# An order of 1,206 words: the H3 and S5 layers of one kernel, scheduled anew

## The chip, the cores and the metric

The kernel runs on one core of a Trainium2 chip. Its five engines work side by side, each through its own queue of instructions in order: TensorE (PE in the profile; its weight loads PEld), VectorE (DVE), ScalarE (ACT), GpSimd (POOL) and SyncE (SP). Transfers are issued from SP (hardware queue q1) and from POOL (software queue q0) and share 16 DMA engines. The metric is the device time of one execution in microseconds; a profile gives the span from the first to the last instruction of one execution.

## The reference

Two layers side by side on inputs of 2048 positions by 1024 channels in bfloat16; their outputs are concatenated.

```python
# A: H3. k is shifted by a filter of 4 taps, multiplied by v, convolved over the sequence
k_shift = sum(k_pad[:, t:t+S, :] * shift_k[:, ks-1-t] for t in range(4))
kv = k_shift * v
y = irfft(rfft(kv, 2*S) * rfft(ssm_k, 2*S))[:S] + kv * ssm_D
a = q * y
# B: S5. a diagonal complex recurrence over the 2048 positions
Lam_bar = exp(dt * Lam);  Bu = x @ (((Lam_bar - 1) / Lam)[:, None] * Bmat).T
for t in range(L):
    h = Lam_bar * h + Bu[:, t, :];  hs.append(h)
b = 2 * (hs @ Cmat.T).real + x * Dskip
return concatenate([a, b], axis=-1)
```

## The kernel before

There is no loop over stages. `ORDER` (lines 69 to 148) is a text of 1,206 words, and the program at the end of `full_kernel` reads them one by one: each calls a small function that issues the instructions of one step. So each engine's queue holds its own steps in the order of the words, with nothing reordered later; a step that waits holds everything behind it on its engine.

```python
for word in ["kv_space"] + ORDER.split():
    task, _, slots = word.partition(":")
    task, _, on[0] = task.partition("@")
    for code, n in re.findall(r"([a-z])(\d+)", slots):
        cur.setdefault(code, []).append(int(n))
    f, *args = task.split(".")
    E[f](*map(int, args))
```

A word has a name and indices, then perhaps `@` with the engine or queue it goes to (`@D` is DVE, `@S` SP, `@G` POOL), then perhaps `:` with the home of the tile it makes: `b` and `a` are slots of SBUF rings (2 and 4 KB a partition), `m` and `e` buffers of products, `w` those of twiddle weights, `p` and `d` are banks of PSUM. A tile that takes a home waits until the last readers of the tile before it are done.

Layer A works as a convolution in three stages through HBM, because the transform is split into 128 x 32 points.

- Start: `ld_w` loads the four taps, eight `wb` (PE) and `wbe` (a copy on ACT or DVE) spread them over the partitions. `hl` loads ssm_k, 512 KB each; `hT` (PE, L637) transposes, `hc` (ACT, L642) copies, `hm` (PE, L650) transforms, `he` (ACT, L657) copies, `hst` stores to Ys_h.
- kv: `kp` loads two rows of k into a ring of eight, `vp` loads v; `kvm`, `kva`, `kvb` and `kvc` (DVE, L590, L604, L609, L611) make kv for two rows; `am` (PE, L617) transforms, `ae` (ACT, L622, tile ysb) copies, `ast` stores to Ys_kv. Each half of 1024 channels of each row is stored by itself: 32 `hst` and 32 `ast`.
- Second stage, 16 groups: `lh` and `lk` load a group of Ys_h and Ys_kv (they cut across all rows, so the first waits for the last store), `lw` the weights; `sh` and `sk` (PE, L685), `she` and `ske` (ACT, L693), `pr` (DVE, L699) the product of spectra, `sa` (PE, L713), `sae` (ACT, L720), `vst` stores to Vs.
- Third stage: `vl` loads Vs, `qp` loads q; `a3` (PE, L742), `a3e` (ACT, L748), `qm` (DVE, L752), `ost` stores the output.

Layer B works on 16 tiles of 128 positions.

- `bl` loads a block of B, `bT` (PE, L464) transposes it and `bc` (ACT L479 or DVE L475) copies it to BT. `cx` loads C and `x` loads x with a transposing DMA, from SP only (L486, L489).
- `U.i.jp.jl` (PE, L498): 16 products of 128 x 128 of tile i; `ue` (ACT, L503) copies; `r1`, `r2`, `sc`, `cm`, `r3`, `r4` (DVE, L512, L524, L529, L534, L512, L541) turn the complex recurrence into a real scan, `sc` being the scan over 2,080 elements; `y.i.half.part` (PE, L552 and L557): the output, eight words a tile; `ye` (ACT, L562), `yst` stores.
- A few small steps (`ld_par`, `sm_pre`, `tabA1`, `sin1`, `stt`, `z1` and others) make the tables of rotations from the parameters. `x.0` to `x.15` and all of C must be in SBUF before the steps that read them; the first half of the sixteen `cx` words (`cx.0` to `cx.3`) is read by `y.i.0`, the second by `y.i.1`.

Of the kernel before, what the change touches and what calls it, by code (L numbers as in the profile page):

```python
# [73 lines left out]
bl.4.0@G:b11 bc.5.0 hm.0.5.0:d2 bT.1.1:p0 par_rest bc.1.1@D hm.0.6.0:d0 sin1 bT.4.1:p1 he.0.5.0:b3 bT.5.1:p0 bc.4.1 bl.0.1@G:b10 tabA2 hm.0.5.1:d1
hT.0.3:p1 bc.5.1 hc.0.3:b13 hl.6@G:a10 hT.0.7:p0 hst.0.5.0@G bT.3.0:p1 bl.7.1@G:b9 hc.0.7:b7 hm.0.1.0:d2 kvm.0:m0 he.0.5.1:b2 bT.6.0:p0 bc.6.0@D
kp.1@G sin2 hst.0.5.1@S kva.0 hm.0.6.1:d1 he.0.6.1:b0 bT.4.0:p0 kp.2@S bc.3.0 x.0:b6 bc.4.0@D eo.1 bT.3.1:p1 kvb.0:a0 hT.0.0:p0 he.0.6.0:b3 bc.3.1
hT.0.2:p1 eo.0 kvc.0 am.0.1:d0 bl.2.0@S:b8 hc.0.2:b4 hc.0.0:b5 kvm.2:m0 bT.7.1:p1 bc.7.1 ld_sd@S hl.5@S:a4 bl.2.1@G:b1 bT.2.1:p0 bc.2.1 bT.0.1:p1
bc.0.1@D hT.0.4:p0 kva.2 cx.5.0 eo.2 ae.0.1:b12 hm.0.7.1:d1 hc.0.4:b11 U.0.2.0:p1 hst.0.6.0@S cx.3.0 stt.0 am.0.0:d0 ae.0.0:b1 U.0.2.1 ue.0.2:a6
kvb.2:a2 U.0.0.0:p0 stt.2 he.0.1.0:b2 bT.2.0:p1 bc.2.0 cx.2.1 hm.0.2.1:d0 hm.0.4.1:d2 he.0.7.1:b9 he.0.4.1:b3 U.0.0.1 ue.0.0 vp.2@S:a7 U.0.3.0:p1
U.0.3.1 U.0.1.0:p0 hm.0.0.1:d1 hm.0.0.0:d2 ast.0.0@G he.0.2.1:b8 kvm.4:m0 cx.4.1 ue.0.3 eo.3 vp.1@S:a1 am.1.0:d0 ast.0.1@S rt U.0.1.1 hst.0.4.1@G  # L80
x.1:b10 U.1.2.0:p1 kp.3@S he.0.0.0:b5 cx.1.1 he.0.0.1:b12 hst.0.0.1@S hst.0.7.1@G stt.3 ue.0.1 am.1.1:d2 hst.0.2.1@S U.1.2.1 z1 ae.1.1:b3 hm.0.7.0:d1
U.1.0.0:p0 kva.4 kvb.4:a0 stt.1 U.1.0.1 ue.1.0:a3 hm.0.2.0:d2 cx.3.1 ue.1.2 z2 ae.1.0:b12 U.1.1.0:p0 U.1.1.1 he.0.7.0:b8 x.4:b7 hm.0.3.0:d0 ue.1.1
hl.7@S:a8 U.1.3.0:p1 U.1.3.1 he.0.2.0:b9 kvc.4 am.5.1:d1 ae.5.1:b1 hl.4@G:a5 hst.0.6.1@G ue.1.3 vp.3@S:a9 kvm.6:m0 kva.6 U.4.1.0:p0 hm.0.3.1:d2
U.4.1.1 ast.1.0@S am.5.0:d1 kvc.2 he.0.3.0:b4 kvb.6:a7 ue.4.1:a1 hst.0.3.0@S x.2:b0 U.4.2.0:p1 U.4.2.1 ae.5.0:b12 ue.4.2 ast.1.1@G hT.1.5:p0
hst.0.0.0@G am.4.1:d0 r1.0:m0 r2.0:a6 kvc.6 am.2.0:d1 U.4.3.0:p1 hst.0.1.0@G hst.0.2.0@S r1.1:m0 sc.0 r2.1:a3 he.0.3.1:b13 hc.1.5:b3 ae.2.0:b5 U.4.3.1
hT.1.7:p0 hst.0.7.0@G ast.5.0@S am.7.0:d1 ue.4.3 hc.1.7:b4 hm.0.4.0:d2 U.2.0.0:p1 cx.7.0 cm.0 ae.7.0:b2 hst.0.3.1@S ae.4.1:b8 ast.5.1@S hT.1.2:p0
am.3.1:d1 U.2.0.1 am.2.1:d0 he.0.4.0:b12 ae.3.1:b11 x.3:b9 kp.4@S ast.3.1@S ast.2.0@G ue.2.0:a9 hst.0.4.0@S hc.1.2:b13 am.3.0:d2 ae.3.0:b1 r3.0:m0
hm.1.5.0:d1 r4.0 U.2.3.0:p1 kvm.8:m0 U.2.3.1 ue.2.3 kva.8 U.2.2.0:p0 sc.1 cx.0.1 hT.1.1:p1 hc.1.1:b5 U.2.2.1 ue.2.2 ae.2.1:b11 am.4.0:d2 ae.4.0:b12
U.3.0.0:p1 U.3.3.0:p0 ast.3.0@S U.3.0.1 cx.7.1 ue.3.0:a2 he.1.5.0:b1 U.3.3.1 ue.3.3 cx.0.0 cx.1.0 hm.1.5.1:d2 hT.1.3:p1 hm.1.1.1:d0 ast.7.0@G
U.2.1.0:p0 hm.1.7.0:d1 U.2.1.1 ast.4.0@S he.1.5.1:b2 hc.1.3:b3 hm.1.3.0:d2 ast.2.1@S he.1.7.0:b12 cx.2.0 ue.2.1 hT.1.4:p1 hm.1.3.1:d1 y.0.0.0:p0  # L90
hc.1.4:b11 hT.1.0:p1 kvb.8:a0 cx.6.1 hst.1.5.1@S he.1.1.1:b3 r1.2:m0 he.1.3.1:b2 r2.2:a9 y.0.0.1 cm.1 hm.1.4.1:d0 y.0.0.2 ast.4.1@S he.1.3.0:b8 cx.5.1
hm.1.4.0:d1 cx.4.0 y.0.0.3 cx.6.0 hc.1.0:b11 hm.1.7.1:d2 he.1.4.1:b4 hst.1.1.1@S r3.1:m0 he.1.7.1:b3 y.0.1.0:p1 y.0.1.1 hm.1.1.0:d0 am.6.0:d2 kp.5@S
y.0.1.2 ye.0.0:b6 hst.1.3.0@S hst.1.7.0@S he.1.4.0:b5 hst.1.4.1@G ae.6.0:b8 hst.1.5.0@G hst.1.7.1@G hm.1.0.0:d1 he.1.0.0:b12 y.0.1.3 ye.0.1 ast.6.0@G
r4.1 hm.1.0.1:d2 hT.1.6:p0 hc.1.6:b4 kvm.10:m0 kva.10 he.1.0.1:b8 kp.6@S hm.1.2.1:d1 y.1.0.0:p1 y.1.1.0:p0 he.1.2.1:b1 y.1.0.1 y.1.1.1 y.1.0.2
am.6.1:d2 hst.1.4.0@S y.1.1.2 am.7.1:d1 ae.7.1:b11 hst.1.0.0@G x.5:b5 y.1.0.3 ye.1.0:b10 yst.0@G y.1.1.3 ye.1.1 x.7:b3 hst.1.3.1@G vp.4@G:a5 kvb.10:a8
U.4.0.0:p1 ae.6.1:b6 vp.6@S:a6 kp.7@S U.5.2.0:p0 kvc.8 am.9.0:d1 ae.9.0:b12 U.4.0.1 U.5.2.1 ue.4.0 kvm.12:m0 kva.12 hm.1.2.0:d2 he.1.2.0:b2 ast.9.0@S
ue.5.2:a10 U.7.3.0:p1 hm.1.6.0:d1 kvb.12:a7 hm.1.6.1:d2 U.7.3.1 ue.7.3:a4 U.5.3.0:p0 he.1.6.0:b13 U.7.0.0:p1 hst.1.2.1@G he.1.1.0:b12 vp.5@S:a3
he.1.6.1:b4 U.5.3.1 U.7.0.1 lw.0@S:w0 kvc.10 am.10.0:d2 lw.1@S:w1 yst.1@G hst.1.2.0@G vp.7@G:a5 am.11.1:d0 ue.7.0 ue.5.3 U.7.2.0:p1 ae.11.1:b1
U.3.2.0:p0 U.7.2.1 kvm.14:m0 kvc.12 ae.10.0:b2 am.10.1:d1 ast.6.1@G ue.7.2 hst.1.1.0@S ast.7.1@S ae.10.1:b6 am.8.1:d0 am.8.0:d2 hst.1.6.0@G ast.11.1@G
ae.8.0:b10 U.3.2.1 ue.3.2 am.12.0:d1 ae.12.0:b13 U.3.1.0:p1 am.12.1:d2 x.6:b11 U.3.1.1 ae.12.1:b12 kva.14 kvb.14:a6 U.5.1.0:p0 ast.10.1@G ld_G@S  # L100
ue.3.1 am.11.0:d1 ae.11.0:b1 U.5.0.0:p1 U.5.1.1 hst.1.6.1@G ae.8.1:b6 kvc.14 hst.1.0.1@G ue.5.1 U.5.0.1 ue.5.0 am.14.0:d2 am.15.0:d0 ae.15.0:b8
ast.11.0@S U.6.1.0:p0 am.9.1:d1 ast.10.0@S ast.12.1@G ast.12.0@G ast.8.1@S ae.14.0:b4 U.6.1.1 ast.8.0@S am.13.1:d0 ue.6.1:a12 U.6.3.0:p1 sc.2 cm.2:a13
r3.2:m0 r4.2 am.15.1:d2 ae.15.1:b12 lh.2@G:a3 ast.15.0@S U.6.3.1 ue.6.3 y.2.0.0:p0 am.14.1:d2 ae.14.1:b1 ast.14.1@S y.2.0.1 lh.0@S:a8 ae.9.1:b2
ast.9.1@S ae.13.1:b13 y.2.1.0:p1 y.2.0.2 y.2.1.1 am.13.0:d0 ast.15.1@S ae.13.0:b10 y.2.0.3 ye.2.0:b6 sh.2.1:d1 ast.13.1@S lh.3@G:a5 sh.3.1:d2
sh.3.0:d0 r1.3:m0 r2.3 sc.3 lh.1@G:a14 she.2.1:a11 ast.14.0@S y.2.1.2 she.3.0:a6 U.7.1.0:p0 x.10:b1 y.2.1.3 ye.2.1 r3.3:m0 cm.3:a7 r4.3 sh.1.0:d1
# [716 lines left out]
```

## Time and profile before

| | |
|---|---|
| median of 3 runs | 376.51 us (366.58 to 381.77) |
| the profiled execution | 366.73 us, span 364.9 us |
| mean granted clock of PE | 0.990 |
| bytes moved | 91.72 MB, 251 GB/s on the mean |
| packets under 512 B (of 65,069) | 37,698 |
| DMA busy share, SP's queue and POOL's | 51.2% and 34.7% |

A row of a timeline or a chain gives start, duration, engine, line, operation, output <- input and count; a bracket at its end gives the engine's idle time before it and what ended that. In the groups of instructions, the numbers behind the bar are busy time in all, mean ns of one, and idle time before with its releasers.

### The profile page before, as it was taken

The numbers are of one execution on the slowest core, as the hardware profiler recorded it, in microseconds if no ns is written. First come the engines' busy times: TensorE is split into PE (matmuls) and PEld (weight loads), VectorE is DVE, ScalarE is ACT, GpSimd is POOL, SyncE is SP. The second block draws the span as 40 slices with busy tenths as digits, with TensorE's granted clock in tenths as the row PEclk, the third lists the DMA queues.
The fourth block names the chain that finished last, engine by engine and source line by source line (L and its number), as shares of the span: only waits on it lengthen the run. The fifth ranks groups of instructions, "written<-read, shape, count | busy, mean of one in ns | idle before, by whom it ended". The sixth has DMA issues, their size and how long they took to land.

```text
span 364.9 us, 9748 instructions
## 1 busy us (share of the span) xinstructions
PE 339.4 (93%) x4237; PEld 220.5 (60%) x4237; DVE 323.7 (89%) x226; ACT 261.0 (72%) x338; POOL 66.4 (18%) x122
## 2 busy tenths in 40 slices
...
GB/s 277 310 340 267 251 248 248 307 309 261 226 365 293 298 217 324 294 245 192 152 254 90 285 186 276 302 343 260 143 133 18 271 175 320 166 341 331 261 280 196
DMA packets 65069, 91.72 MB, mean 251 GB/s; under 512 B 37698, under 2 KB 41410, under 8 KB 65026
## 3 DMA queue, kind: packets, MB, share of 16 engines
q1 hardware_dynamic: 53666, 51.76, 51.2%
q0 software_dynamic: 11360, 39.33, 34.7%
...
## 4 chain that ended last, share of the span: by engine, by line
PE 49%; DVE 17%; DMA 16%; ACT 9%; issue 6%; POOL 1%; ACTq 0%; POOLq 0%; DVEq 0%; SPq 0%
PE ps_y L552 19%; PE ps_u L498 18%; DVE mt L590 5%; DMA Ys_h<-ysbh 4%; DMA Ys_kv<-ysb 4%; PE ps_a L713 3%; PE ps_a L685 3%; ACT ysbh L657 3%; DVE mt L512 2%; DVE h L529 2%; DMA wts<-a_c_W 2%; PE ps_a L742 2%; DMA l2k<-Ys_kv 2%; DVE mt L604 2%; DMA Vs<-vsb 2%
## 5 line engine op out<-in xcount | busy, mean ns | idle before, releaser
L498 PEld LDWEIGHTS <-BT 128*128 128x128 bf16 x2048 | 119.0, 98 | 20.5 <-issue 11.8
L498 PE MATMUL ps_u<-xT,BT 128*128 128x128 bf16 x2048 | 126.9, 220 | 0.4 <-DMA xT<-in_B_x_dram 0.2
L552 PE MATMUL ps_y<-CT,h 128*128 128x512 bf16 x512 | 125.9, 380 | 1.2 <-ACT ysbh L657 1.2
L552 PEld LDWEIGHTS <-h 128*128 128x128 bf16 x512 | 44.2, 98 | 50.3 <-issue 9.7
L529 DVE TENSOR_TENSOR_SCAN h<-rtab,h 128x2080 bf16<-128x2080 f32 x16 | 71.8, 4486 | 0.2
L503 ACT CAST u<-ps_u 128x512 bf16<-128x512 f32 x64 | 38.3, 601 | 16.2 <-PE ps_u L498 15.3
L562 ACT CAST yo<-ps_y 128x512 bf16<-128x512 f32 x32 | 19.0, 593 | 37.7 <-PE ps_y L552 33.6
L622 ACT CAST ysb<-ps_a 128x1024 bf16<-128x1024 f32 x32 | 32.2, 1037 | 12.6 <-PE ps_a L617 7.9
L699 DVE TENSOR_TENSOR hab<-x,h 128x4096 bf16<-128x4096 bf16 x16 | 36.6, 2288 | 4.5 <-ACT x L693 2.1
L720 ACT CAST vsb<-ps_a 128x1024 bf16<-128x1024 f32 x32 | 31.6, 1023 | 8.3 <-PE ps_a L713 8.3
L512 DVE TENSOR_TENSOR mt<-u,Z 128x4096 bf16<-128x4096 bf16 x16 | 36.6, 2290 | 0.7
L590 DVE TENSOR_TENSOR mt<-kring,wbc 128x2048 bf16<-128x2048 bf16 (+3 forms) x14 | 35.8, 2593 | 1.6 <-DMA kring<-in_A_k_dram 1.6
L512 DVE TENSOR_TENSOR mt<-h,Z 128x4096 bf16<-128x4096 bf16 x16 | 36.7, 2291 | 0.3
L657 ACT CAST ysbh<-ps_a 128x1024 bf16<-128x1024 f32 x32 | 32.5, 1043 | 4.3 <-DMA Ys_kv<-ysb 2.4
L693 ACT CAST x<-ps_a 128x1024 bf16<-128x1024 f32 x32 | 31.8, 1025 | 4.0 <-PE ps_a L685 3.8
L693 ACT CAST h<-ps_a 128x1024 bf16<-128x1024 f32 x32 | 31.5, 1023 | 1.6 <-PE ps_a L685 1.5
L557 PE MATMUL ps_y<-Dd,xT 128*128 128x128 bf16 x128 | 28.1, 219 | 0.0
L650 PE MATMUL ps_a<-hT,F1t 128*128 128x512 bf16 x64 | 20.8, 405 | 3.8 <-ACT ysb L622 3.2
L524 DVE TENSOR_TENSOR h<-mt 128x2048 bf16<-128x2048 bf16 x16 | 19.5, 1220 | 1.4 <-PE ps_y L552 1.1
L173 POOL DMA_DIRECT2D Ys_h<-ysbh x18 | 12.9, 719 | 41.7 <-ACT ysbh L657 41.3
L557 PEld LDWEIGHTS <-xT 128*128 128x128 bf16 x128 | 12.5, 98 | 13.0
L541 DVE TENSOR_TENSOR h<-mt 128x2048 bf16<-128x2048 bf16 x16 | 19.6, 1223 | 0.4
...
## 6 DMA issues: line engine op xcount, KB each, us to landing
Ys_kv<-ysb SPq DMA_DIRECT2D x21, 256.0 KB, 4.8
...
Ys_h<-ysbh POOLq DMA_DIRECT2D x18, 256.0 KB, 5.3
...
Ys_h<-ysbh SPq DMA_DIRECT2D x14, 256.0 KB, 4.6
...
```

Of the source, the lines that this page charges most:

```text
L498: nc.tensor.matmul(pu[:, w, jl, :], BT[:, 2 * jp + jl, w, d, :], xT[:, d, :], start=(d == 0), stop=(d == ND - 1))
L503: nc.scalar.copy(u[:, :, 2 * jp:2 * jp + 2, :], st["pu", i, jp][:])
L512: nc.vector.tensor_mul(m, s_, w_)
L529: nc.vector.tensor_tensor_scan(gf, rtab[:].rearrange("p a j t -> p (a j t)"), gf, 0.0, ALU.mult, ALU.add)
L552: nc.tensor.matmul(py[:], h[:, 1 - w, j, 2:TP], CT[:, j, w, dh * 512:(dh + 1) * 512], start=(j == 0 and w == 0), stop=(j == NJ - 1 and w = ...
L557: nc.tensor.matmul(py[:, dl * P:(dl + 1) * P], st["xT", i][:, d, :], Dd[:, d, :], start=False, stop=False)
L590: nc.vector.tensor_mul(m[:, :, j0:j0 + n, :], a_, wbc[:, j0:j0 + n, :].unsqueeze(1).to_broadcast([P, 2, n, DV]))
L622: nc.scalar.copy(st["ysb", r, u][:], st["pa", r, u][:].rearrange("p e d -> p (e d)"))
L657: nc.scalar.copy(st["yh", f, rp, u][:], st["pa", f, rp, u][:])
L693: nc.scalar.copy(t_[:, c_, :], st["ps", key, gq, c_][:].rearrange("p e d -> p (e d)"))
L699: nc.vector.tensor_mul(st["m2", gq][:], st["x16", gq][:].unsqueeze(2).to_broadcast([P, 2, 2, D]), st["h16", gq][:].unsqueeze(1).to_broadca ...
L720: nc.scalar.copy(vsb[:, gi, :], st["ps", "v", gq][gi][:].rearrange("p e d -> p (e d)"))
```

## The change

Nothing but the text in `ORDER` differs. Both orders hold the same 1,206 words without their engines, queues and homes, so the same products, copies and transfers are made; the places in the order, the `@` and the `:` change. POOL issued 110 of the transferring words and SP 152; after, it is 92 and 170. Among the copies that may go to DVE, seven `bc` and four `wbe` were there; after, five and two. The first loads are others, and ld_w goes from POOL to SP:

```diff
-bl.0.0@S:b1 ld_w@G:a0a3 bT.0.0:p0 wb.7:p1 bc.0.0@D bl.7.0@S:b2 wbe.7@D wb.0:p0 bl.6.1@S:b0 wbe.0@D bT.7.0:p1 bc.7.0@D bT.6.1:p0 ld_par par_T:p1 p32
-hl.0@G:a2 bc.6.1 hl.1@G:a1 exp1 hl.3@G:a6 wb.1:p1 wbe.1@D wb.3:p0 wbe.3 wb.5:p1 wbe.5 bl.1.0@S:b3 bl.3.0@G:b6 dve2 bl.5.1@G:b7 exp2 kp.-1@G hl.2@S:a7
...
+bl.4.0@S:b1 ld_F@G bl.5.1@S:b0 bT.4.0:p1 bc.4.0 bl.3.0@S:b2 bT.5.1:p0 bT.3.0:p1 bc.3.0 bc.5.1@D ld_par par_T:p0 p32 exp1 dve2 bl.7.0@G:b5 ld_w@S:a1a0
+wb.2:p0 hl.1@S:a4 dve3 sm_pre wbe.2 wb.1:p1 wbe.1 wb.5:p0 bl.0.1@S:b6 wbe.5 wb.3:p1 wbe.3 wb.7:p0 wbe.7 sin0 exp2 bl.4.1@G:b7 bT.4.1:p1 bc.4.1
+bT.0.1:p0 bc.0.1 wb.6:p1 rt wbe.6 bT.7.0:p0 bc.7.0 bl.1.0@G:b8 bl.6.1@G:b4 kp.-1@G tabA1:a5a2a7a6 hl.3@S:a9 tabA2 hl.2@S:a3 hl.0@S:a10 hT.0.1:p1
+hc.0.1:b3 hT.0.6:p0 hc.0.6:b9 hT.0.3:p1 hm.0.6.0:d0 cx.1.1 hT.0.2:p0 hc.0.3:b10 hm.0.3.1:d1 hm.0.3.0:d2 bT.6.1:p1 sin2 par_rest hc.0.2:b13 bc.6.1@D
+wb.4:p0 wb.0:p1 wbe.4@D kp.0@S he.0.3.1:b1 bl.0.0@G:b0 sin1 vp.0@S:a1 wbe.0@D kvm.0:m0 bl.5.0@S:b2 he.0.6.0:b7 bl.6.0@G:b11 bT.1.0:p0 kp.1@S bc.1.0
```

The loads on SP around `kp.3` to `kp.5` (the words of other engines between them left out; this is a list of words, not of lines):

```diff
-kp.3@S cx.1.1 hst.0.0.1 hst.0.2.1 cx.3.1 x.4 hl.7 vp.3 ast.1.0 hst.0.3.0 x.2 hst.0.2.0 ast.5.0 cx.7.0 hst.0.3.1 ast.5.1 x.3 kp.4
-ast.3.1 hst.0.4.0 cx.0.1 ast.3.0 cx.7.1 cx.0.0 cx.1.0 ast.4.0 ast.2.1 cx.2.0 cx.6.1 hst.1.5.1 ast.4.1 cx.5.1 cx.4.0 cx.6.0 hst.1.1.1 kp.5
+kp.3@S ast.2.1 hst.0.0.0 cx.7.1 cx.7.0 ast.0.1 hst.0.7.0 cx.5.0 ast.0.0 hst.0.0.1 hst.1.5.0 hst.1.5.1 ast.3.0 cx.4.0 ast.4.0 cx.6.0 cx.5.1 cx.6.1 ast.4.1 cx.3.0 cx.1.0 cx.2.0 cx.3.1 kp.4
+ast.5.0 ast.5.1 x.3 kp.5
```

The last lines, where one tile of y stood behind `r4.14` with another, and now `y.15` stands alone behind `r4.15`:

```diff
-vl.5.1@S:a14 ost.1.1@S y.11.1.2 y.13.0.0:p0 a3e.2.0:a7 a3e.2.1 yst.8@G y.11.1.3 ye.11.1 y.13.0.1 vl.5.0@S:a8 y.13.1.0:p1 vl.6.0@G:a13 vl.6.1@G:a1
...
-a3e.0.0:a2 yst.11@S qm.2 ost.2.1@G y.14.1.3 ye.14.1:b1 y.15.1.0:p0 y.14.0.0:p1 y.15.1.1 y.14.0.1 y.15.1.2 ost.2.0@G a3e.5.1 qm.5 ost.5.0@S ost.5.1@G
-y.14.0.2 a3e.0.1 y.15.1.3 qm.0 ye.15.1 ost.0.1@S ost.0.0@S yst.15@S ost.3.1@G y.14.0.3 ye.14.0 yst.14@S
...
+y.14.1.3 ye.14.1 r4.15 a3.6.1:d0 ost.0.0@S ost.1.0@S yst.13@S yst.14@S y.15.1.0:p1 a3e.3.1 qm.3 ost.3.1@S y.15.0.0:p0 y.15.1.1 ost.1.1@G a3e.6.1
+y.15.0.1 ost.5.1@G y.15.1.2 y.15.0.2 y.15.1.3 y.15.0.3 ye.15.1:b2 qm.6 ost.6.1@S yst.7@S ost.6.0@S ost.3.0@G ye.15.0 yst.15@S
```

Between these, `sc.2` stands ahead of `kvc.14` instead of behind it; `x.9` stands ahead of the last `ast` words and `x.10` behind `lk.2`, where both stood just ahead of `lk.2`; and the words of U, y, sh, sk, sa and pr are interleaved otherwise, with other slots.

144 lines of the change are left out of this document (71 added, 73 removed).

## The prediction

> **What bounds the kernel now.** I read the page's busy line first, then the same engines cut at the places where the work changes, then the chain of waits.
>
> ```profile
> span 364.9 us, 9748 instructions
> PE 339.4 (93%) x4237; PEld 220.5 (60%) x4237; DVE 323.7 (89%) x226; ACT 261.0 (72%) x338; POOL 66.4 (18%) x122
> ```
>
> ```profile
> core 0: us, PE busy (x) PEld busy (x) DVE busy (x) ACT busy (x) POOL busy (x), PEclk, DMA share, GB/s
> 0.00:25.00 25.00, 17.20 (x110) 10.62 (x111) 16.03 (x50) 16.42 (x27) 12.58 (x28) 1.00 0.90 306
> 25.00:100.00 75.00, 65.34 (x793) 51.03 (x791) 74.05 (x55) 67.57 (x92) 8.55 (x17) 0.95 1.08 267
> 100.00:165.00 65.00, 63.62 (x672) 41.76 (x672) 59.88 (x32) 43.89 (x56) 15.41 (x25) 1.00 0.99 290
> 165.00:344.00 179.00, 178.36 (x2578) 110.21 (x2579) 167.84 (x87) 124.92 (x155) 26.01 (x47) 1.00 0.72 224
> 344.00:365.00 21.00, 14.87 (x96) 6.86 (x94) 5.86 (x5) 8.17 (x11) 3.89 (x7) 0.98 0.86 237
> ```
>
> The windows' columns are the stretch, its length, then busy us (instructions) of PE, PE's weight loads, DVE, ACT and POOL, then granted clock, DMA share and GB/s. PE's idle time is length less busy: 7.8 us up to 25, 9.7 from 25 to 100, 1.4 from 100 to 165, 0.6 from 165 to 344, 6.1 behind that; 25.6 in all. From 100 on PE has no gap that counts, while DVE is idle for 5.1 + 11.2 us there. That this busy time is work shows in the chain (start, us, engine, tile, line, count):
>
> ```profile
> 290.27 9.04 PE ps_u L498 x160
> ...
> 355.20 3.68 PE ps_y L552 x17
> ```
>
> 160 products of U run at 9.04/160 = 56.5 ns each and 17 of y at 216 ns, back to back. So a U word (16 products) costs PE 0.90 us and a y word (four products and half the time two short ones) about 0.92. The program does the same products in both orders, so the span is PE's work, 339.4, plus PE's idle time, 25.6. A gain has to come out of the 17.5 us of idle before 100 or the 6.1 at the end; a loss is any new gap. DMA share is about 1 from 25 to 165 and 0.72 after: up to 165 loads and stores are the second limit. The profiled execution took 366.73 us, 1.8 more than its span. The median shown is 376.51 (366.58 to 381.77), so runs spread 4% and the profiled one is near the fastest; I sum against 366.73.
>
> **Part 1, the start.** Before, the first product of the DVE stream, kvm.0, begins at
>
> ```profile
> 25.07 4.42 DVE L590 TENSOR_TENSOR mt<-kring,wbc 128x8192 bf16<-128x8192 bf16 x1
> ```
>
> and the first hT words at
>
> ```profile
> 16.76 1.93 PE L637 MATMUL ps_t<-ident,hk 128*128 128x128 bf16 x16 [1.53 <-ACT wbc L479]
> ```
>
> held there by a scale copy on ACT, not by the four hl tiles. After, hl.1 is the tenth load on SP, with hl.3, hl.2 and hl.0 the 12th to 14th, behind four bl tiles. Words up to hl.0 carry 5.0 MB; at the 306 GB/s of the first window plus 1.5 us of start that is 18 us. Two of the eight wb products (4 and 0), which kvm.0 needs, now stand behind four hT words.
>
> ```profile
> L475 DVE COPY BT<-ps_t 128x1024 bf16<-128x1024 bf16 x7 | 4.8, 689 | 5.1 <-PE ps_t L464 5.1
> ...
> L475 DVE CAST wbc<-ps_a 128x512 bf16<-128x512 f32 x4 | 2.7, 686 | 1.8 <-PE ps_a L415 1.8
> ...
> L479 ACT CAST wbc<-ps_a 128x512 bf16<-128x512 f32 x4 | 2.3, 578 | 0.7 <-PE ps_a L415 0.6
> ...
> L479 ACT COPY BT<-ps_t 128x1024 bf16<-128x1024 bf16 x9 | 9.1, 1040 | 7.0 <-PE ps_t L464 7.0
> ...
> L642 ACT COPY hT<-ps_t 128x1024 bf16<-128x1024 bf16 x16 | 16.3, 1038 | 1.8 <-PE ps_t L637 1.8
> ...
> L415 PE MATMUL ps_a<-hk,ones 1*128 1x512 bf16 x8 | 4.5, 589 | 2.0 <-DMA hk<-in_A_shift_k_dram 1.3 <-DVE p L273 0.3 <-DVE BT L475 0.2
> ```
>
> From 18: one hT at about 1 us, then ACT's four hc copies and a sine of like size one after another (5 x 1.04), then wb.4 and wb.0 at 0.59 and the copy wbe.0 at 0.69: 26.1, with handoffs 26.5. kvm.0 is **1.4 us later** (bounds: 2 earlier, if the hl tiles land by 14.5; 5 later, if POOL's 2.9 MB share the engines evenly and the copies queue). On DVE, bc words fall from seven to five and wbe words from four to two: 4 x 0.69 = 2.8 us leave DVE, all ahead of kvm.0; 2 x 1.04 + 2 x 0.58 = 3.2 go to ACT, which is busy 67.6 of 75 us from 25 to 100. DVE's relief buys nothing while PE is the bound. vp.0 takes slot a1, which the scale row holds until wb.0 is done, so SP stands from about 9 to 26 us with x.0, kp.1 and everything else behind it; POOL's bl loads cover most of that, and I charge nothing, with 3 us as the other end (in-flight bytes end near 23).
>
> **Part 2, kvm.0 to kvc.14** (the last product of the kv path). I counted DVE words between the two in both orders: eight each of kvm, kva, kvb and kvc, three bc, four stt, three r1 and r2, two r3 and r4, all alike; only the scans differ, two before and three after (sc.2 moved ahead). Prices:
>
> ```profile
> L529 DVE TENSOR_TENSOR_SCAN h<-rtab,h 128x2080 bf16<-128x2080 f32 x16 | 71.8, 4486 | 0.2
> ...
> L512 DVE TENSOR_TENSOR mt<-u,Z 128x4096 bf16<-128x4096 bf16 x16 | 36.6, 2290 | 0.7
> ...
> L604 DVE TENSOR_TENSOR mt<-mt 128x4096 bf16<-128x4096 bf16 x8 | 18.3, 2290 | 0.1
> ...
> L590 DVE TENSOR_TENSOR mt<-kring,wbc 128x8192 bf16<-128x8192 bf16 x4 | 17.7, 4423 | 1.6 <-DMA kring<-in_A_k_dram 1.6
> ...
> L524 DVE TENSOR_TENSOR h<-mt 128x2048 bf16<-128x2048 bf16 x16 | 19.5, 1220 | 1.4 <-PE ps_y L552 1.1
> ...
> L609 DVE TENSOR_TENSOR acc<-mt 128x2048 bf16<-128x2048 bf16 x8 | 9.8, 1221 | 0.3
> ...
> L368 DVE SCALAR_TENSOR_TENSOR Z<-tab,nbi 128x128 bf16<-128x128 f32 x8 | 2.8, 350 | 0.0
> ```
>
> So +4.5. Against it stand the two waits for loads of before (last bracket of each row: idle and releaser) and the end of kvc.14:
>
> ```profile
> 103.41 4.42 DVE L590 TENSOR_TENSOR mt<-kring,wbc 128x8192 bf16<-128x8192 bf16 x1 [1.36 <-DMA kring<-in_A_k_dram]
> ...
> 114.42 1.22 DVE L611 TENSOR_TENSOR acc<-acc,v 128x2048 bf16<-128x2048 bf16 x1 [2.94 <-DMA v<-in_A_v_dram]
> ...
> 133.94 1.23 DVE L611 TENSOR_TENSOR acc<-acc,v 128x2048 bf16<-128x2048 bf16 x1
> ```
>
> 1.36 + 2.94 = 4.3 could go since DVE comes later, but kp.5 and vp.4 stand at nearly the same place among the bytes (27.6 and 31.3 MB, against 28.1 and 32.3) and vp.7 later (37.8 against 36.0). I keep half: -2.2. New is bc.2.1 on DVE ahead of kvm.2: its bank is freed by hc.0.4, eleven ACT pieces behind hc.0.2 (24.2 + ten at 1.04 and one of 1.8 = 36.4), then a transpose at 0.9 and handoffs: 37.7, where DVE is at 26.5 + 9.7 = 36.2, so +1.5. kvc.14 ends 1.4 + 4.5 - 2.2 + 1.5 = **5.2 later**, at 140.4 (bounds +1.3 and +15, the second from the rival below).
>
> Moved past on SP are the transposing loads. Between kp.3 and kp.4 stand 11 of them and 11 stores, where before 6 and 10 stood, and between kp.4 and kp.5 1 and 2 where 9 and 8 stood:
>
> ```profile
> 47.16 3.63 SPq L486 DMA_TRANSPOSE CT<-in_B_C_im_dram  x1
> ...
> 77.25 0.57 SPq L172 DMA_DIRECT2D kring<-in_A_k_dram  x1
> ...
> 84.25 3.64 SPq L486 DMA_TRANSPOSE CT<-in_B_C_re_dram  x2
> ...
> 98.83 0.40 SPq L172 DMA_DIRECT2D kring<-in_A_k_dram  x1
> ```
>
> Before, kp.4 to kp.5 (77.25 to 98.83) took 21.6 us for 9 transposes and 8 stores, so 22 transfers of this mix take 26.4. kp.3 waits for hl.4, which waits for r1.0; DVE's words from 26.5 to there sum to 34.8, plus the 1.5, so r1.0 ends at 62.8, kp.3 issues at 63.5, kp.4 at 89.9, and lands 4.6 later (98.83 to 103.41 for kp.5) at 94.5. DVE gets to kvm.8 by a further 34.0 us, at 96.8. Covered by 2.3 us; no charge.
>
> **Part 3, kvc.14 to the first sk.** The transforms of the last kv rows end like this before:
>
> ```profile
> 139.72 1.93 ACT L622 CAST ysb<-ps_a 128x1024 bf16<-128x1024 f32 x2 [0.28 <-PE ps_a L617]
> ...
> 150.21 1.01 ACT L622 CAST ysb<-ps_a 128x1024 bf16<-128x1024 f32 x1 [1.33 <-PE ps_a L617]
> ```
>
> The two copies at 139.72 wait for PE (ps_a, L617), which had kvc.14 since 135.17; two am words at 0.43 (the row of 84.58 in the fence below) put PE there at 138.9, so kvc.14 had 3.7 us of slack. That leaves 5.2 - 3.7 = 1.5. From kvc.14 to the last ysb copy PE has 5 U, 7 am and 5 y words before (12.1 us), and 7 U, 5 am, 4 y and 2 sh after, as ae.15.1 now stands behind ye.2.1 (12.7): +0.6. Every lk load waits for the last store:
>
> ```profile
> 84.58 0.43 PE ps_a L617 x2
> ...
> 157.69 7.24 DMA l2k<-Ys_kv
> ...
> 164.98 0.63 PE ps_a L685 x16
> ```
>
> and sk starts as it lands (a sk or sh word: 0.31). Here x.9 and x.10 stood on SP before lk.2; after, x.9 is earlier and x.10 behind lk.2, but lk waited for the stores, so nothing is won. Ahead of the first sk PE has 64 U, 26 y and 8 sh words instead of 60, 32 and 5: +3.6 - 5.5 + 0.9, so 1.0 us less is done when it waits. PE is behind by 1.5 + 0.6 + 1.0 = **3.1 us**.
>
> **Part 4, the rest and the end.** From 165 to 344 PE idles 0.6; the order can't win there, and could lose some tenths at each of 13 further pr; 0 taken, 4 as the upper bound. At the end one y tile follows r4.15 instead of two (7.4 us instead of 14.9): that frees DVE, which has 11.2 + 15.1 us to spare, and PE's last y, its copy and the last store cost 6.1 as before. Queues: 18 transfers go from POOL to SP (110 and 152 become 92 and 170).
>
> ```profile
> Ys_h<-ysbh POOLq DMA_DIRECT2D x18, 256.0 KB, 5.3
> ...
> Ys_h<-ysbh SPq DMA_DIRECT2D x14, 256.0 KB, 4.6
> ```
>
> POOL's stores of this tile land 5.3 us after issue, SP's 4.6, as a store that nobody waits for: no price either way. The Trainium skill, SBUF — State Buffer, "Who interferes with whom", says that transfers issued from GpSimd can be starved while DVE holds the shared port and that the hardware queue is immune; by it the move would gain. These rows show 0.7 us of it at most; by the rule at its best the load waits still charged would go too, 2.2 us less.
>
> **Sum:** 366.7 + 3.1 = 369.8 us, PE 3.1 later from the first sk to the end.
>
> **Rivals.** *Slower: the transposes in front of kp.4.* At 47.16 one took 3.63 us to issue and at 84.25 two took 3.64; if eleven in a row back up to 2.9 each, the stretch is 11 x 2.9 + 11 x 0.45 = 36.9, kp.4 lands at 105 and DVE waits 8.2 at kvm.8. Less slack already spent, all 8.2 reach the first sk, with y.0.0 (needs cx.3.1) late on PE meanwhile: 369.8 + 8.2 = 378.0. It decides once the eleven take over 2.2 us each on average (1.95 in the 26.4 above). For: DMA share 1.08 from 25 to 100. Against: 21.6 us for 17 transfers. *Faster: U fills PE's early gaps.* Ahead of kvm.6 stand 28 U words instead of 16, ahead of kvm.8 32 instead of 25. If they fill the 9.7 us idle from 25 to 100 and the delays of parts 1 to 3 hide in it, 366.7 - 9.7 + 1.0 = 358.0. Against: PE's words there wait for ACT's copies of the banks, and ACT has 7.4 us left, 3.2 of it taken. *No effect of the order* (every engine finds the same waits): 366.7, inside the forecast's band.
>
> **Numbers.** 2% of 366.7 is 7.3, about what a measurement of this kernel can tell: 359.4 to 374.0 counts as the same. Forecast and no effect 0.50, slower rival 0.33, faster rival 0.17; so faster 0.17, same 0.50, slower 0.33. The forecast's own range is 364 to 374 (kvc.14 early; 4 us in part 4). The range for 8 in 10 is 359 to 380: it takes in the slower rival, and the upper half of the runs' spread shown.
>
> **What would show it.** Right: first DVE kvm (L590) near 26.5; no kring wait at kvm.8; kvc.14's end near 140; the first L685 on l2k near 168; PE idle under 1 us from there to the end. Wrong: a kring wait of over 3 us near 97 (slower rival); PE idle from 25 to 100 under 5 us (faster); a first sk before 163; or PE gaps in the pr stretch, which no row of before shows.

## The result and the profile after

The changed kernel takes 371.58 us in the median of 17 runs (370.17 to 374.33), the kernel before 368.65 in the median of 17 runs beside it (365.18 to 381.77). The ratio is 1.0105, with a 95% interval of 1.0075 to 1.0135: 3.9 us slower on 368.65, less than the 2% that the prediction took as the least that can be told, but told all the same. The two medians as they stand differ by 2.9. The profiled execution took 370.17 us with a span of 368.1, 3.2 more than before. Some executions of both kernels are disturbed and some per cent longer: the ratios leave them out, the medians do not, and of the disturbed traces that e12 and e14 left only the first 25 us of e12 are read.

The page's busy line, and the same stretches as before (columns as in the prediction; the last stretch ends behind the span):

```profile
span 368.1 us, 9738 instructions
...
PE 338.0 (92%) x4237; PEld 219.6 (60%) x4237; DVE 320.4 (87%) x222; ACT 266.9 (73%) x344; POOL 55.3 (15%) x103
```

```profile
core 0: us, PE busy (x) PEld busy (x) DVE busy (x) ACT busy (x) POOL busy (x), PEclk, DMA share, GB/s
0.00:25.00 25.00, 12.97 (x81) 8.54 (x82) 11.57 (x43) 16.81 (x22) 7.57 (x21) 1.00 0.97 272
25.00:100.00 75.00, 65.91 (x790) 50.47 (x788) 69.52 (x54) 70.27 (x100) 7.24 (x12) 0.98 1.01 256
100.00:165.00 65.00, 62.37 (x737) 44.14 (x736) 62.28 (x33) 47.58 (x59) 13.33 (x23) 1.00 0.94 297
165.00:344.00 179.00, 178.77 (x2522) 108.25 (x2520) 164.58 (x87) 124.15 (x153) 23.50 (x41) 1.00 0.74 223
344.00:369.00 25.00, 18.00 (x117) 8.25 (x115) 12.43 (x7) 8.09 (x11) 3.66 (x6) 0.97 0.86 258
```

PE's work fell by 1.4 us and its idle time rose by 4.5, from 25.6 to 30.1. By stretch (length less busy time; the last one to the end of the span): 12.0 us up to 25 (7.8 before), 9.1 from 25 to 100 (9.7), 2.6 from 100 to 165 (1.4), 0.2 to 344 (0.6), 6.1 behind it (6.1). So the loss stands in two places: +4.2 at the start and, from 100 on, 2.6 where before there was only the 1.2 us wait for the first load of lk. DVE has lost its full stretch from 25 to 100 (69.5 busy instead of 74.05) and made that up later, where it had room.

PE's timeline, the rows with the four gaps that matter (start, duration, engine, line, operation and count; in the bracket the idle time ahead and its releaser):

```profile
15.92 1.03 PE L464 MATMUL ps_t<-ident,ld 128*128 128x128 bf16 x8 [4.66 <-DMA ld<-in_B_B_im_dram]
...
21.35 1.93 PE L637 MATMUL ps_t<-ident,hk 128*128 128x128 bf16 x16 [2.28 <-DMA hk<-in_A_ssm_k_dram]
...
103.46 0.59 PE L650 MATMUL ps_a<-hT,F1t 128*128 128x512 bf16 x2 [1.83 <-ACT ysbh L657]
...
113.56 1.05 PE L498 MATMUL ps_u<-xT,BT 128*128 128x128 bf16 x16 [0.80 <-ACT u L503]
```

At 15.92 PE has waited 4.66 us for bl.0.1, at 21.35 another 2.28 for the hl tiles. The three hT words at the start are done at 24.5; before they were at 18.7 (one at 14.22, which the prediction overlooked, and the two of its row at 16.76). At 103.46 and 113.56 it waits for copies of ACT. From there on PE has no gap that counts, not even at the first sk. In the chain of waits the load of lk lands just as PE gets to it:

```profile
162.82 6.63 DMA l2k<-Ys_kv
169.49 0.41 PE ps_a L685 x8
```

DVE's timeline, SP's and ACT's at the places that the prediction named:

```profile
27.68 0.69 DVE L475 COPY BT<-ps_t 128x1024 bf16<-128x1024 bf16 x1 [10.59 <-PE ps_t L464]
...
30.69 4.43 DVE L590 TENSOR_TENSOR mt<-kring,wbc 128x8192 bf16<-128x8192 bf16 x1
...
101.83 4.42 DVE L590 TENSOR_TENSOR mt<-kring,wbc 128x8192 bf16<-128x8192 bf16 x1 [2.69 <-DMA kring<-in_A_k_dram]
...
143.13 1.20 DVE L611 TENSOR_TENSOR acc<-acc,v 128x2048 bf16<-128x2048 bf16 x1
```

```profile
7.17 9.87 SPq L486 DMA_TRANSPOSE CT<-in_B_C_im_dram  x1
...
29.52 0.33 SPq L172 DMA_DIRECT2D v<-in_A_v_dram  x1
...
67.85 0.69 SPq L172 DMA_DIRECT2D kring<-in_A_k_dram  x1
...
95.41 0.58 SPq L172 DMA_DIRECT2D kring<-in_A_k_dram  x1
96.03 0.90 SPq L173 DMA_DIRECT2D Ys_kv<-ysb  x2
105.22 1.24 SPq L489 DMA_TRANSPOSE xT<-in_B_x_dram  x1
```

```profile
102.40 2.84 ACT L657 CAST ysbh<-ps_a 128x1024 bf16<-128x1024 f32 x3 [3.33 <-DMA Ys_kv<-ysb]
```

kvm.0 begins at 30.69, held by bc.6.1, whose transpose stands behind three hT words on PE, and by the scale copies behind that. SP issues cx.1.1 for 9.87 us, with kp.0 behind it until 17.09, and then stands until vp.0's slot is free at 29.52. kp.4 is issued at 95.41, behind the eleven transposing loads, and DVE waits 2.69 us for it at kvm.8 (101.83). The two stores behind kp.4 (ast.5.0 and ast.5.1, 96.03) land late as well: ACT's next copy, he.1.0.0, goes into slot b7, which ast.5.0 empties, and waits 3.33 us for that. Here PE's gap of 1.83 at 103.46 comes from.

### The profile page after: what moved, and what is told of

Same layout as the page of the kernel before. It is cut to its first block, busy times and chain, and to the rows that moved or that the text cites. A ratio compares the mean times of both kernels' runs of the same rounds, so it can differ in the third digit from the quotient of the medians.

```text
span 368.1 us, 9738 instructions
## 1 busy us (share of the span) xinstructions
PE 338.0 (92%) x4237; PEld 219.6 (60%) x4237; DVE 320.4 (87%) x222; ACT 266.9 (73%) x344; POOL 55.3 (15%) x103
## 4 chain that ended last, share of the span: by engine, by line
PE 60%; DMA 14%; issue 10%; DVE 7%; ACT 5%; SPq 2%; POOL 1%; POOLq 0%; ACTq 0%; DVEq 0%
PE ps_u L498 23%; PE ps_y L552 22%; PE ps_a L685 4%; PE ps_a L713 3%; PE ps_a L617 3%; DMA ld<-in_B_B_im_dram 3%; DMA out_dram<-ot 3%; DVE h L529 2%; DMA Ys_h<-ysbh 2%; DMA l2k<-Ys_kv 2%; DVE hab L699 2%; DMA vv<-Vs 2%; DMA Ys_kv<-ysb 2%; PE ps_a L742 2%; DVE mt L512 2%
## 5 line engine op out<-in xcount | busy, mean ns | idle before, releaser
L552 PE MATMUL ps_y<-CT,h 128*128 128x512 bf16 x512 | 129.6, 380 | 0.4 <-ACT hT L642 0.2
L562 ACT CAST yo<-ps_y 128x512 bf16<-128x512 f32 x32 | 18.9, 590 | 28.6 <-PE ps_y L552 26.4
L650 PE MATMUL ps_a<-hT,F1t 128*128 128x512 bf16 x64 | 19.8, 399 | 4.6 <-ACT ysbh L657 4.6
L464 PE MATMUL ps_t<-ident,ld 128*128 128x128 bf16 x128 | 12.3, 258 | 11.7 <-DMA ld<-in_B_B_im_dram 4.7
L173 POOL DMA_DIRECT2D Ys_h<-ysbh x11 | 7.9, 719 | 83.1 <-ACT ysbh L657 82.7
```

What stands on the lines that cost most here:

```text
L552: nc.tensor.matmul(py[:], h[:, 1 - w, j, 2:TP], CT[:, j, w, dh * 512:(dh + 1) * 512], start=(j == 0 and w == 0), stop=(j == NJ - 1 and w = ...
```

## The experiments

Every kernel was timed in five rounds beside the kernel before, whose median was 368.4 in e1 to e4, 368.7 in e5 to e8, 370.8 in e9 to e12 and 368.2 in e13 and e14. Differences in us are therefore taken between ratios, times 368.5; the changed kernel stands at 1.0105. The intervals are 0.7 to 1.4% wide, so a difference of less than some 2 us to the changed kernel can't be told: -0.6, +0.6, 0.0 and -1.5 in the last column are such. The expectations name these theories. L: the loss is PE's wait for late loads at the start. A: it is the copies moved from DVE to ACT, which bounds PE from 20 to 60. S: it is SP's queue ahead of kp.4. D: the end follows DVE's lateness. P: PE is the only bound from 114 on, and only its own gaps count. Q: it is the stores queued behind kp.4.

| run | edit | ratio to before, 95% | against the changed kernel |
|---|---|---|---|
| e1 | four loads behind hl.0 on SP | 1.0022 [0.9981, 1.0062] | -3.1 us |
| e2 | four bc words to DVE | 1.0190 [1.0133, 1.0246] | +3.1 |
| e3 | kp.4, ast.5 up SP's queue | 1.0184 [1.0137, 1.0230] | +2.9 |
| e4 | vp.0 behind x.1 | 1.0108 [1.0071, 1.0145] | +0.1 |
| e5 | kp.4 on POOL | 1.0020 [0.9986, 1.0054] | -3.1 |
| e6 | ast.5 on POOL | 1.0202 [1.0144, 1.0260] | +3.6 |
| e7 | two bc words to DVE | 1.0090 [1.0044, 1.0136] | -0.6 |
| e8 | e1, e5, e6 and three words to DVE | 1.0104 [1.0045, 1.0163] | 0.0 |
| e9 | e1 and e5 | 0.9979 [0.9942, 1.0016] | -4.6 |
| e10 | kp.4 behind ast.5 on SP | 1.0219 [1.0149, 1.0288] | +4.2 |
| e11 | sc.2 behind kvc.14 | 1.0122 [1.0052, 1.0192] | +0.6 |
| e12 | kernel before, three hl tiles late | 1.0067 [1.0014, 1.0120] | +2.5 against before |
| e13 | e1, and kp.4 on SP ahead of cx.7.1 | 1.0064 [1.0028, 1.0101] | -1.5 |
| e14 | kp.4 on SP ahead of cx.7.1 | 1.0101 [1.0059, 1.0143] | -0.1 |

**e1, the loads of the start.**

```diff
 hl.0@S:a10
+kp.-1@S bl.0.0@S:b0 bl.6.0@S:b11 bl.2.0@S:b12
...
-kp.-1@G
-bl.0.0@G:b0
-bl.6.0@G:b11
-bl.2.0@G:b12
```

> The changed kernel with four loads (kp.-1, bl.0.0, bl.6.0, bl.2.0; 1.57 MB) taken from POOL's queue and put on SP right behind hl.0, so that they no longer share the DMA engines with the four hl tiles. Theory L (the loss is PE's wait for late loads at the start): at 290 GB/s 1.57 MB are 5.4 us, so bl.0.1 lands near 12 instead of 15.9 and the first hT stands near 17 instead of 21.35; PE's idle time in 0 to 25 falls from 12.0 by about 4 to that of before (7.8), and the time falls by 3 to 4 us against the changed kernel (371.6), to about 368. Theory A (ACT's copies bound PE from 20 to 60, and the changed kernel gave ACT 3.2 us more of them): PE's idle time only moves from 0-25 to 25-60 and the time stays within 1 us of 371.6. Theory S (SP's queue further on, the eleven transposing loads ahead of kp.4): no change at all, 371 to 372.

The time fell by 3.1 us, the way theory L had it. PE's timeline and DVE's in e1:

```profile
16.49 0.58 PE L415 MATMUL ps_a<-hk,ones 1*128 1x512 bf16 x1 [2.80 <-ACT BT L479]
...
19.78 1.92 PE L637 MATMUL ps_t<-ident,hk 128*128 128x128 bf16 x16 [1.36 <-ACT wbc L479]
...
29.06 4.43 DVE L590 TENSOR_TENSOR mt<-kring,wbc 128x8192 bf16<-128x8192 bf16 x1
```

No gap of PE waits for bl.0.1 or an hl tile any more; what it waits for now is ACT's chain of copies (2.80 and 1.36). The first hT is 1.6 us earlier, kvm.0 too (29.06). Theory S alone, by which the start was without effect, is out. PE keeps that lead, 1.8 us at the row of 113.56 (111.72 here). The profiled execution of e1 took 370.61, 2 us above e1's median of 368.64; it loses the lead again in waits that the changed kernel's trace does not have, 1.32 us for weights at 185.83 and 1.99 for Vs at 352.85. So the trace shows 1.6 of the 3.1 us, and the rest stands on the times alone; e9 less e5 gives 1.5 for the same four loads and e13 less e14 1.4, neither clear of noise by itself. The loads are worth 1.5 to 3 us, and what is left of the 4.2 lost at the start stays with ACT's copies.

**e2, four copies from ACT to DVE.**

```diff
-bc.0.1
+bc.0.1@D
...
-bc.7.0
+bc.7.0@D
...
-bc.1.0
+bc.1.0@D
...
-bc.0.0
+bc.0.0@D
```

> The changed kernel with four copies of transposes (bc.0.1, bc.7.0, bc.1.0, bc.0.0) done by DVE instead of ACT: 4 x 1.04 leave ACT, 4 x 0.69 go to DVE. Theory A (ACT bounds PE from 20 to 60): PE's idle time from 0 to 60 falls by 3 to 4 and the time by as much, to about 368; DVE's kvm.0 is later by up to 2 and kvc.14 too, which costs nothing. Theory L (late loads): PE waits as long for bl.0.1 and for hl.0; the time falls by under 1 us. If DVE's lateness is what carries the loss (theory D), the time grows by 2 to 3 us.

3.1 us slower, which theories A and L both had wrong. PE's timeline shows why:

```profile
36.16 1.05 PE L464 MATMUL ps_t<-ident,ld 128*128 128x128 bf16 x16 [2.23 <-DVE BT L475]
```

bc.1.0 and bc.0.0 stand behind kvm.0 on DVE, so the banks of their transposes come free only after its 4.4 us; PE stands for 2.23 us. The edit tells where a copy may not go and not what ACT costs; e7 was made for that.

**e3, kp.4 and ast.5 further up.**

```diff
+ast.5.0@S ast.5.1@S kp.4@S
 cx.6.0
...
-kp.4@S
...
-ast.5.0@S ast.5.1@S
```

> The changed kernel with kp.4 and the two stores ast.5.0 and ast.5.1 moved up SP's queue, ahead of the last seven of the eleven transposing loads (cx.6.0 and what follows). Theory S: kp.4 issues near 84 instead of 95.4, the 2.7 us wait at kvm.8 goes, slot b7 comes free earlier, so ACT's 3.3 us wait near 102 and PE's 1.83 us gap at 103.5 go too: time 1.5 to 2 us less, near 370. If DVE's wait for kp.4 is what the end follows (theory D), 2.7 us less, near 369. Theories L and A alone: under 0.5 us.

2.9 us slower. The wait at kvm.8 went (99.78, no wait), but SP is served in order: its row of the stores took 7.08 us, waiting for a copy that ACT made at 90, and the cx loads stood behind it. SP's timeline, and PE's at its y words:

```profile
84.33 7.08 SPq L173 DMA_DIRECT2D Ys_kv<-ysb  x3
```

```profile
96.54 0.59 PE L552 MATMUL ps_y<-CT,h 128*128 128x512 bf16 x1 [4.28 <-DVE h L529]
```

PE stood for 4.28 us, put down to DVE's scan; that had ended 0.5 us earlier, while the first of the held cx loads had left SP only 4.6 us before. That it was the cx load fits these rows and isn't shown by more.

**e4, the blocked queue.**

```diff
-vp.0@S:a1
...
 x.1@S:b9
+vp.0@S:a1
```

> The changed kernel with vp.0 (whose slot a1 is held by the scale row until wb.0 is done) moved on SP from behind kp.0 to behind x.1, so that SP no longer stands from 18 to 29.5 us with bl.5.0, kp.1, bl.2.1, bl.1.1, vp.2, x.0 and x.1 behind it. If the blocked queue costs time, the DMA hole of 185 to 238 GB/s between 18 and 36 us fills, x.0 and x.1 issue 10 us earlier, and PE's idle time from 25 to 60 falls by 1 to 3 us with the time. If it costs nothing, as the prediction charged (ACT's copies hold PE there anyway), the time stays within 0.5 us of 371.6, and vp.0 itself, landing near 36, may make DVE wait at kvc.0.

No change (1.0108 and 1.0105). Without vp.0 SP took 8.36 us over the next two bl loads, whose slots were still taken:

```profile
19.23 8.36 SPq L172 DMA_DIRECT2D ld<-in_B_B_im_dram  x2
```

The cost of nothing that the prediction put on vp.0 stands.

**e5, kp.4 alone, from POOL.**

```diff
-kp.4@S
+kp.4@G
```

> The changed kernel with kp.4 issued from POOL, which stands idle there, instead of from SP behind the eleven transposing loads. The 2.7 us wait at kvm.8 goes and DVE runs 2.7 us earlier from 99 to 143. Theory P (from 113 on PE is the only bound and DVE's lateness costs nothing): time within 0.5 us of the changed kernel's 371.6, PE's 1.83 us gap at 103.5 stays. Theory D (the end follows DVE): 2.7 us less, about 369.

One word moved to another queue takes 3.1 us off. Theory P had expected 0.5 at most, theory D 2.7, with PE's gap still there; but PE's gaps went. POOL's timeline, ACT's and the windows of e5:

```profile
60.41 0.55 POOL L172 DMA_DIRECT2D kring<-in_A_k_dram  x1
```

```profile
98.85 1.01 ACT L657 CAST ysbh<-ps_a 128x1024 bf16<-128x1024 f32 x1
```

```profile
100.00:165.00 65.00, 65.00 (x773) 45.48 (x772) 64.33 (x35) 49.19 (x61) 13.32 (x23) 1.00 0.95 298
```

kp.4 leaves at 60.41 and not at 95.41; the stores ast.5 land 5.3 us after their issue instead of 8.2 at the most, with no kp load among them (vp.3, 512 KB from POOL at 97, is there in both); he.1.0.0 starts at 98.85 and not at 102.40; PE's idle time from 100 to 165 is 0.0 instead of 2.6. These rows fit a price that kp.4 took from PE through the stores beside it. Whether it was that or DVE's wait, e5 can't tell, since both went; e10 was made for it. That the gaps belong to kp.4 and not to one execution, other traces bear out: from 100 to 115 PE idles 2.4, 1.5, 2.2 and 2.9 us in e1, e4, e7 and e11, which leave kp.4 on SP as the change has it (2.6 in the changed kernel), and 0.0 in e5 and 0.2 in e9, which issue it from POOL.

**e6, the two stores from POOL.**

```diff
-ast.5.0@S
-ast.5.1@S
+ast.5.0@G
+ast.5.1@G
```

> The changed kernel with the stores ast.5.0 and ast.5.1 issued from POOL instead of from SP behind the eleven transposing loads and kp.4; nothing waits on SP for them. Slot b7 comes free some 8 us earlier, so ACT's 3.3 us wait near 102 and PE's gap of 1.83 at 103.5 go. Theory P (every gap of PE counts in full): 1.8 us less, about 369.8. Theory D (the end follows DVE, whose wait for kp.4 stays): under 0.5 us.

3.6 us slower where 1.8 faster was expected. ACT's wait went (its copy at 99.07). But on SP x.3 had waited behind kp.4 until slot b1 was emptied by ast.5.1 (105.22 in the changed kernel); with that slot free, x.3, kp.5 and a store left within 4 us of kp.4. SP's timeline, DVE's and PE's:

```profile
96.48 0.58 SPq L172 DMA_DIRECT2D kring<-in_A_k_dram  x1
97.23 1.39 SPq L489 DMA_TRANSPOSE xT<-in_B_x_dram  x1
98.72 2.00 SPq L172 DMA_DIRECT2D kring<-in_A_k_dram  x1
```

```profile
105.68 4.42 DVE L590 TENSOR_TENSOR mt<-kring,wbc 128x8192 bf16<-128x8192 bf16 x1 [6.44 <-DMA kring<-in_A_k_dram]
```

```profile
112.38 1.50 PE L498 MATMUL ps_u<-xT,BT 128*128 128x128 bf16 x16 [4.37 <-DMA xT<-in_B_x_dram]
```

kp.4, issued at 96.48, reached DVE at 105.68, 9.2 us later, and PE waited 4.37 us for x.3. A Ys_h store that left in this stretch was late too, and ACT stood longest of all:

```profile
117.92 1.01 ACT L657 CAST ysbh<-ps_a 128x1024 bf16<-128x1024 f32 x1 [9.90 <-DMA Ys_h<-ysbh]
```

The store that it waits for was issued at 100.82. From 102 to 110 the DMA engines were busy throughout (share 1.09) and yet moved only 97 GB/s, where the changed kernel moved 192 at a share of 0.66; why, this trace doesn't tell. So the rate fell as well as the order of the transfers changing, and the 3.6 us can't be split between the two. The wait that was taken away had kept x.3 and kp.5 apart from kp.4.

**e7, only the two copies that stand ahead of kvm.0.**

```diff
-bc.0.1
+bc.0.1@D
...
-bc.7.0
+bc.7.0@D
```

> The changed kernel with only bc.0.1 and bc.7.0 on DVE, the two copies that stand ahead of kvm.0 where DVE waits 10.6 us anyway; the two that stood behind kvm.0 in the run before this stay on ACT. 2.08 us leave ACT at 17 to 21. Theory A (ACT's copies bound PE from 20 to 60): PE is 1.5 to 2 us earlier at 60, time about 369.8. Theory L (loads: bl.0.1 lands at 15.9, hl.0 at 21.3): the first hT still stands at 21.3, ACT is only idle longer ahead of it, time within 0.5 us of 371.6.

1.0090, inside the changed kernel's interval: no change that can be told. Theory A, that the pieces moved from DVE to ACT are the loss, isn't needed; the edit moves two of the bc words, with the loads still late.

**e8, all of these together.** It holds the edits of e1, e5, e6 and e7, with wbe.6@D.

> The changed kernel with all of these: kp.-1, bl.0.0, bl.6.0 and bl.2.0 on SP behind hl.0; kp.4, ast.5.0 and ast.5.1 on POOL; bc.0.1, bc.7.0 and wbe.6 on DVE. With the loads in order ACT's chain of copies comes next (PE waited 2.80 and 1.36 us for it at 16.5 and 19.8), and these three words take 2.6 us off it. Theory P with L and A: 3 (loads) + 1.8 (gap at 103.5) + 1.5 (copies), so about 365.5, below the kernel before (368.4). If PE's earlier finish runs into the loads of lk at the first sk (1.5 us of wait there in the run with the loads in order), about 367.

1.0104, the changed kernel's own ratio, in six runs from 367.3 to 373.1. Its profiled execution (367.31, span 365.4) was the shortest of these, its median not. What in it gives back 4 us wasn't found; the edit of ast.5 that e6 shows to harm is in it, so e9 was made without it. The wait of 1.5 us at the first sk of e1 that the expectation charges isn't there: e1 waits 0.28 us at its first sk (167.86), and 1.32 at 185.83 for weights.

**e9, the two edits that gave 3 us each.** The edits of e1 and of e5.

> The changed kernel with the two edits that each gave 3 us: kp.-1, bl.0.0, bl.6.0 and bl.2.0 on SP behind hl.0, and kp.4 issued from POOL. If the late loads at the start and kp.4 behind the transposing loads are two separate losses on PE, they add: 371.6 - 3.0 - 3.0 = 365.6, 3 us below the kernel before (368.7). If both only fill the same slack ahead of the first sk (whose load then ends last: in the run with the loads in order PE waited for it again), the time stays near 368.

4.6 us, not 6.2. The median is 367.59 beside 370.84 for the kernel before; the ratio 0.9979 reaches past 1, so it is as fast as the kernel before and can't be called faster. The 6.2 counted e1 at its 3.1; against e5 the four loads bring 1.5 here, near the 1.6 of e1's own trace, so no loss between the two edits has to be explained. There is a gap in this trace all the same, in PE's timeline and ACT's:

```profile
68.72 0.59 PE L617 MATMUL ps_a<-acc,F1t 128*128 128x512 bf16 x2 [1.52 <-ACT ysbh L657]
```

```profile
66.75 1.01 ACT L622 CAST ysb<-ps_a 128x1024 bf16<-128x1024 f32 x1 [1.99 <-DMA Ys_h<-ysbh]
```

kp.4 now leaves at 58.25, among the Ys_h stores, and ACT waits 1.99 us for one of them. But that kp.4 makes this gap isn't shown. In e5 it leaves at 60.41 and PE has no such gap, and in e11, where kp.4 leaves on SP as in the changed kernel, the same word of PE has it:

```profile
71.30 0.59 PE L617 MATMUL ps_a<-acc,F1t 128*128 128x512 bf16 x2 [1.17 <-ACT ysbh L657]
```

There too ACT waits for a Ys_h store (1.64 us at 69.32). The gap comes and goes between executions; its cause is open. ACT's wait near 102 isn't gone for good either: with kp.4 away from there, ACT still waits 1.65 us for its Ys_kv store in e9 (99.77) and 2.02 in e13 (102.60), of the 3.33 in the changed kernel.

**e10, kp.4 one place further down, behind the stores.**

```diff
-kp.4@S
...
 ast.5.0@S ast.5.1@S
+kp.4@S
```

> The changed kernel with kp.4 moved on SP from ahead of the stores ast.5.0 and ast.5.1 to right behind them: 1 us later on the queue, so DVE's wait at kvm.8 grows from 2.7 to about 3.7, while the stores leave 0.6 us earlier and have the DMA engines to themselves. Theory Q (the loss was the stores behind kp.4: slot b7 late, ACT waits, PE's gaps of 1.83 and 0.80 at 103 to 114): the gaps shrink to under 1 in all and the time falls by 1.5 to 2.5 us, to about 369.5. Theory D (the loss was DVE's wait for kp.4, carried to the end): 1 us more, about 372.5.

4.2 us slower, against both. SP's, ACT's, DVE's and PE's rows:

```profile
97.21 0.73 SPq L172 DMA_DIRECT2D kring<-in_A_k_dram  x1
100.72 2.01 SPq L489 DMA_TRANSPOSE xT<-in_B_x_dram  x1
```

```profile
99.61 1.01 ACT L657 CAST ysbh<-ps_a 128x1024 bf16<-128x1024 f32 x1 [0.20 <-DMA Ys_kv<-ysb]
```

```profile
106.07 4.42 DVE L590 TENSOR_TENSOR mt<-kring,wbc 128x8192 bf16<-128x8192 bf16 x1 [6.97 <-DMA kring<-in_A_k_dram]
```

```profile
128.98 0.59 PE L617 MATMUL ps_a<-acc,F1t 128*128 128x512 bf16 x2 [4.49 <-DVE acc L611]
```

Theory Q's mechanism fits: ACT waits 0.20 for the store instead of 3.33, and the gap of 1.83 is gone. But kp.4 was issued 1.8 us later and landed 8.9 after that, beside x.3; DVE waited 6.97 and was 4.2 later at kvm.8 than in the changed kernel, and PE then stood 4.49 us for DVE's acc. DVE's lateness does count once it is large enough: 4.2 plus the 1.7 that PE was earlier (gaps of 0.41 and 0.54 instead of 1.83 and 0.80) gave a wait of 4.5, so the changed kernel had some 1.4 us of slack left there (an estimate from these rows).

**e11, sc.2 where it was before the change.**

```diff
-sc.2
...
 kvc.14
+sc.2
```

> The changed kernel with the scan sc.2 put back behind kvc.14 on DVE, as it stood before the change. kvc.14 ends 4.5 us earlier, near 139.8; the last ysb copy, the stores behind it and the loads of lk follow earlier, by up to 4. The prediction charged PE 1.5 us for kvc.14's delay: if that is right, the time falls by 1.5 us, to about 370. Theory P (PE has no gap from 114 to the end, so nothing on DVE there counts): within 0.5 us of 371.6; the first sk finds its load earlier and does not start earlier.

1.0122 against 1.0105: nothing won. kvc.14 ended at 142.05 instead of 144.33:

```profile
140.82 1.23 DVE L611 TENSOR_TENSOR acc<-acc,v 128x2048 bf16<-128x2048 bf16 x1 [0.51 <-DMA v<-in_A_v_dram]
```

That is 2.3 us earlier and not 4.5, since in this execution kvm.8 was 1.15 later and kvc.14 waited 0.51 for its load. This execution had also lost 1.17 us at 71.30 and reached the row of 113.56 at 115.05, so the +0.6 is no price of sc.2. Theory P holds for this as far as the noise allows: nothing is won by an earlier kvc.14.

**e12, the converse in the kernel before.**

```diff
-hl.0@G:a2
-hl.1@G:a1
-hl.3@G:a6
...
 bl.4.1@G:b9
+hl.0@G:a2 hl.1@G:a1 hl.3@G:a6
```

> The kernel before, with hl.0, hl.1 and hl.3 moved on POOL's queue behind kp.-1 and four bl loads (1.83 MB, about 6 us at 300 GB/s), which is what the change did to the hl tiles. Theory L (the hl tiles' landing sets PE's start): the first hT starts near 20 instead of 14.2 to 16.8, PE's idle time in 0 to 25 grows from 7.8 to about 11, the time from 368.5 to about 371.5. If before's start has cover that the changed kernel lacks, the time stays within 1 us of 368.5.

2.5 us slower than before (interval 0.5 to 4.4). Its first hT word, in PE's timeline:

```profile
17.08 0.44 PE L637 MATMUL ps_t<-ident,hk 128*128 128x128 bf16 x2 [3.01 <-DMA hk<-in_A_ssm_k_dram]
```

It waits 3.01 us for an hl tile, where before none waited for one. Two further waits of 0.82 and 0.63 follow, and up to 25 PE idles 10.6 us instead of 7.8. So late hl tiles alone, with the first hT at 17.08 and not at 21.35 as in the changed kernel, cost time in the other kernel too; the interval is too wide to say what part of the 4.2 they are.

**e13 and e14, kp.4 early but on SP.**

```diff
+kp.4@S
 cx.7.1
...
-kp.4@S
```

> The changed kernel with the four loads on SP behind hl.0 and kp.4 kept on SP but ahead of the first of the eleven transposing loads, so that it issues near 70 instead of 58 (POOL) or 95 (the change). If the 2 us that the two edits together lacked were lost because kp.4, issued at 58, shared the DMA engines with the Ys_h stores that ACT then waited for (1.99 us, PE's gap of 1.52 at 68.7), that gap goes and the time is 365.5 to 366.5, about 2.5 us below the kernel before. If something else ends last, it stays at 367.5.

> The changed kernel with only that move of kp.4 on SP, ahead of the first of the eleven transposing loads. If kp.4's place in the order is the cause, whatever queue issues it, PE's gaps at 103 to 114 go and the time is near 368.6, as with kp.4 on POOL. If it was the relief of SP's queue, it stays near 371.6.

e14 is where the changed kernel is (1.0101), e13 1.4 us better than that and 3.1 worse than e9. The 1.5 by which e13 is ahead of the changed kernel isn't clear of noise. So moving kp.4 up on SP isn't shown to gain anything. e13's SP, ACT and PE rows:

```profile
72.00 0.50 SPq L172 DMA_DIRECT2D kring<-in_A_k_dram  x1
```

```profile
81.84 1.01 ACT L622 CAST ysb<-ps_a 128x1024 bf16<-128x1024 f32 x1 [2.02 <-DMA Ys_kv<-ysb]
```

```profile
83.39 1.95 PE L498 MATMUL ps_u<-xT,BT 128*128 128x128 bf16 x32 [1.62 <-ACT u L503]
```

At 72.00 kp.4 goes out right behind two stores; ACT then waits 2.02 us for a Ys_kv store, and PE 1.62 for ACT. A wait stands 7 to 10 us behind kp.4 in the changed kernel (102), in e13 (82) and in e9 (67), but e11 has the last of these with kp.4 elsewhere, and e5 has none, so that it follows kp.4 isn't shown. Whether e5 gained by POOL's queue as such or by the moment at which kp.4 leaves, these runs don't tell: no run issues it from SP near 60, or from POOL near 95.

## Why the prediction came out as it did

The time forecast, 369.8, lies 0.4 below the profiled 370.17 and 1.8 below the median, and the direction of its sum (+3.1, with +3.2 measured in the span and +3.9 by the ratio) is right. Yet it called this no change that can be told, and the parts of its sum are not those that the trace shows: that the sum comes so near is luck.

**The step that failed first: part 1.** The prediction wrote the span as PE's work and PE's idle time, then costed the late loads only through kvm.0 on DVE and gave PE's own idle time at the start no term. That is where 4.2 us arose. Bringing four loads earlier takes 3.1 back by e1's times (1.6 by its trace, 1.5 and 1.4 by e9 and e13), and late hl tiles cost the other kernel 2.5 (0.5 to 4.4, e12). The size of the delay was also short: hl.0 was put at 18 us from 5.0 MB of words up to it, and PE waited for it until 21.35. POOL's queue had by 7.3 us issued three more bl loads (0.79 MB) that stand later in the order but share the engines, and at the window's 272 GB/s the 5.8 MB are 21.3 us; the prediction had POOL's bytes only in its upper bound. kvm.0 came 5.6 later instead of 1.4, 0.6 beyond the upper bound. Right were the costs of nothing for vp.0 (e4) and for the pieces moved between DVE and ACT (e7, two of the bc words).

**The second: kp.4 "covered by 2.3 us; no charge" in part 2.** The stretch from kp.3 to kp.4 took 27.6 us, with 26.4 forecast (26.9, had its prices per transfer been fitted to the whole 21.6 us of before), and the eleven transposes 1.5 us each (16.3 us of SP's rows in all), well under the 2.2 at which the slower rival was to decide. But kp.3 itself was 4.35 late (much of it kvm.0's delay beyond the forecast, 4.2) and kp.4's landing took 6.4 us instead of 4.6, while DVE was only 2.3 late at kvm.8: 4.35 + 1.2 + 1.8 - 2.3 = 5.0, and the cover of 2.3 became a wait of 2.7. The rival had the right place at a third of its price. What neither saw is the way to PE: through ACT, which waits for the stores behind and beside kp.4 (3.33 us, 0.20 in e10 and none in e5), and through DVE's wait only beyond some 1.4 us more (e10). By e5 kp.4's place and queue are worth 3.1 us together; which of the two stays open, as do the waits that e9 and e13 keep for such a store. The rest of part 2 came out: from kvm.0 to the end of kvc.14 113.6 us, 113.9 forecast, though the wait charged at bc.2.1 (1.5) didn't occur and the two waits for k made 3.0.

**The third: part 3's 3.1 us.** kvc.14 ended 9.2 later, at 144.33, and PE still had no gap over 0.25 us between 113.56 and its last y; e11 moved it by 2.3 and won nothing. The three terms (1.5, 0.6, 1.0) were charged where PE, late by itself, had other words to do. The first sk was put near 168 and began at 169.49, its load landing at 169.45.

**How it adds up.** Gains the sum didn't hold make the difference: the wait at the first sk (1.20 before) is gone, idle time from 25 to 100 is 0.6 less, PE's busy time 1.4 less. 4.2 (start) + 2.6 (the gaps at 103 to 114) - 1.2 - 0.6 - 0.6 (other idle time from 100 to 344) - 1.4 = 3.0, and 0.2 of rounding, for the 3.2 of the spans.

**Part 4 and the rivals.** No loss from 165 to the end: right (0.2 idle, then 6.1 as before). U did not fill the early gaps: 9.1 us of idle from 25 to 100, where the faster rival needed under 5. On the queues, the rows of the Ys_h stores after, and in e5:

```profile
Ys_h<-ysbh SPq DMA_DIRECT2D x21, 256.0 KB, 4.3
...
Ys_h<-ysbh POOLq DMA_DIRECT2D x11, 256.0 KB, 6.6
```

```profile
Ys_h<-ysbh SPq DMA_DIRECT2D x21, 256.0 KB, 5.7
...
Ys_h<-ysbh POOLq DMA_DIRECT2D x11, 256.0 KB, 6.0
```

The Trainium skill, SBUF — State Buffer, "Who interferes with whom", has transfers issued from GpSimd starved while DVE holds the shared port. After, the POOL stores take 2.3 us longer than SP's, which agrees in direction. But in e5, with one load more on POOL, the two differ by 0.3, and of the moves between the queues one to POOL gained 3.1 (kp.4) and one to POOL lost 3.6 (ast.5): the queue alone doesn't set these times, and the rows of e6 and e10 point to what else is in flight.
